# Attention with soft experts on one core: the products p·v done per tile of 128 rows, or once per batch

## The chip, the cores and the metric

The kernel runs on one core of a Trainium2 chip. The metric is the device time of one execution in microseconds, the median of three runs. Everything is in one program: eight batches, one launch.

## The reference, cut to what matters

Two stages follow each other. The first is a retention layer with 8 heads, whose output (576 tokens of 512 values in each of 8 batches) is the input `x` of the second; the second has 4 experts, each an attention head of its own with 64 columns:

```
for e in range(E):                       # E = 4 experts
    q = x @ wq[e]; k = x @ wk[e]; v = x @ wv[e]
    scores = scale * (q @ k.transpose(0, 2, 1))      # causal
    a = exp(scores - max); a /= a.sum(-1) + 1e-09
    ye = a @ v @ wo[e]
    out += (weights of the 2 experts that the gate picks, per token) * ye
```

The change concerns `a @ v`: for each token row the weighted sum of `v` over all tokens up to it, for four experts, in fp32.

## The kernel before, in words

A batch of 576 tokens is cut into five tiles `t` of 128, 128, 128, 128 and 64 rows (`CH`), and for the projections into two ranges `r` (`RNG`): tiles 0 and 1, and tiles 2 to 4. A main loop runs over `n`, one tile of the retention stage in each turn; the tile of the expert stage that a turn works on is `m = n - 6`, so the two stages overlap. In each turn the engines get, in this order:

- the retention products of tile `n` and the end of tile `n - 1` (`qk`, `old`, `own`, `st`: products of 64x64 blocks, four at a time on quarters of the array);
- `scores(m)` (L331, L338): products into PSUM, and `soft`: VectorE subtracts, masks and takes the row maximum (`nm`, L349, L353), ScalarE takes the exponential and its row sum (L357);
- `gates` (L285 to L304), small VectorE instructions once a range, when a range's `vproj` is done;
- `spread(m)`: VectorE and ScalarE scale the rows by sum and gate (L378, L376), and VectorE transposes them in blocks of 32x32 (L382) into `pth`, from where TensorE can stream them;
- `work(n)`: of the table `STEPS` what is due in this turn: the projections `kq0`, `kq1` (`pj`, L230), `v0`, `v1` (`pv`, L255, which also send v through DRAM into the layout `vq`), and the output products `o0`, `o1` (`po`, L430) of the two ranges;
- `values(m - 1)` (L399): for each 32 tokens `j` of the keys, for the two experts `z` in a half and the four 32-row groups `g`, one product with 64 columns of `vq` as the weights and the 32 or 64 columns of one tile of `pth` streamed. Each such product is on the chip two products with their own weight loads, as the others in fp32 are. Eight of them lie on different parts of the array (four row groups, two column halves).

`values` then gathers its four PSUM banks into `y32` (ScalarE L413, VectorE L411), and GpSimd splits that into a rounded part `yh` (L419) and a rest `yl` (L420), which `outproj` reads. For tile `t` there are 32, 64, 96, 128 and 144 products in the program, 464 a batch.

TensorE, VectorE, ScalarE and GpSimd run their instructions in the order in which the program writes them. PSUM is a ring of eight banks taken in that order. Counted by `n`, the five kinds of turn, called steps A to E below, hold:

| step | n | expert tile t | work before | values before |
|---|---|---|---|---|
| A | 5b + 6 | 0 | kq1 of batch b | tile 4 of batch b - 1 |
| B | 5b + 7 | 1 | v1 of b, o1 of b - 1 | tile 0 of b |
| C | 5b + 8 | 2 | kq0 of b + 1 | tile 1 of b |
| D | 5b + 9 | 3 | o0 of b | tile 2 of b |
| E | 5b + 10 | 4 | v0 of b + 1 | tile 3 of b |

After the loop `end` does the last tiles, whose scores, spreads, values and output products follow each other with little else beside them.

Of the kernel before, what the change touches and what calls it, by code (L numbers as in the profile page):

```python
# [8 lines left out]
F32 = mybir.dt.float32  # L9
# [24 lines left out]
def kernel(ctx: ExitStack, tc: tile.TileContext, xf, xt, vkf, vkt,  # L34
# [165 lines left out]
    def fetch(n):  # L200
        o, kc, w = WCUT[n]
        RAW[n] = raw = ld.tile([128, kc, w], F32, name="raw", bufs=3)
        nc.sync.dma_start(raw, wraw[:, o:o + kc * w].rearrange("p (k w) -> p k w", k=kc))
# [105 lines left out]
    SS, PT, YU = {}, {}, {}  # L309
# [52 lines left out]
    def spread(m):  # L362
# [9 lines left out]
        PT[m] = pth = sb.tile([128, ws[-1] // 32, n, 32], F32, name="pth", tag="pth", bufs=2)  # L372
# [12 lines left out]
    def values(m):  # L385
        b, t = divmod(m, 5)
        t0, C = CH[t]
        r = 0 if t < 2 else 1
        r0, n, tiles = RNG[r]
        pth = PT.pop(m)  # L390
        k = C // 64
        nj = (t0 + C) // 32
        py = [bank([128, k, 32], "ys") for g in range(4)]
        for j in range(nj):
            vq, jj = VN[b, 0 if j < 8 else 1][2], j - (0 if j < 8 else 8)
            i0 = 1 if k == 2 and j >= nj - 2 else 0
            for z in range(2):
                for g in range(4):
                    mm(py[g][HALF[z], i0:], vq[QUAD[g], jj, D * z:D * z + D], pth[QUAD[g], j, k * z + i0:k * z + k],  # L399
                       start=(j == 0), stop=(j == nj - 1))  # L400
        if (b, r) not in YU:
            YU[b, r] = (sb.tile([128, 2, n], F32R, name=f"yh{r}", bufs=1),
                        sb.tile([128, 2, n], F32R, name=f"yl{r}", bufs=1))
        yh, yl = YU[b, r]
        l0 = t0 - r0
        hi, lo = yh[:, :, l0:l0 + C], yl[:, :, l0:l0 + C]
        y32 = sb.tile([128, 2, k, 2, 32], F32, name="y32", tag="y32")
        for g in range(4):
            o = y32[:, g // 2, :, g % 2]
            if g % 2:  # L410
                v.tensor_copy(o, py[g])  # L411
            else:
                act(o, py[g], AF.Copy)  # L413
        y32 = y32.rearrange("p a i b c -> p a (i b c)")
        if m == NC - 3:
            act(hi, y32, AF.Copy)
            v.tensor_sub(lo, y32, f(hi))
        else:
            gp.tensor_copy(hi, y32)  # L419
            gp.tensor_sub(lo, y32, f(hi))  # L420

    def outproj(b, r, d):
        r0, n, tiles = RNG[r]
        yh, yl = YU[b, r]
# [15 lines left out]
    for b in range(B):  # L440
        late = b == B - 1

        for n, kind in ((5 * b + 3, "kq0"), (5 * b + 5 - late, "v0"), (5 * b + 6, "kq1"), (5 * b + 7, "v1"),
                        (5 * b + 9 + (b == B - 2), "o0"), (5 * b + 12, "o1")):
            if b or kind[-1] == "1" or kind == "o0":
                STEPS.setdefault(n, []).append((b, kind, None))

# [3 lines left out]
    def work(n):  # L451
        for b, kind, part in STEPS.get(n, []):
            r = int(kind[-1])
# [21 lines left out]
    def end():  # L475
# [4 lines left out]
        values(LAST + 1)  # L480
# [23 lines left out]
    for n in range(NC + 2):  # L504
# [6 lines left out]
        new, old = TILES.get(n, []), TILES.get(n - 1, [])  # L511
# [89 lines left out]
```

## Time and profile before

| | us |
|---|---|
| median of three runs | 598.53 |
| lowest and highest of them | 595.57, 599.73 |
| the profiled execution, its time | 601.69 |
| its span, first to last instruction | 599.8 |
| TensorE products busy in it | 495.3 |
| VectorE busy | 344.3 |
| ScalarE busy | 261.8 |
| GpSimd busy | 213.7 |

The time of an execution is 1.9 us more than the span. Busy time of TensorE is the time in which at least one product is in flight; eight small ones at once count once. The granted clock is the share of its full 2.4 GHz that TensorE gets; it takes two levels, 1.0 and 0.5, and a slice or stretch shows their mean.

### The profile page before, as it was taken

What the parts mean: (1) busy time and instruction counts of PE and PEld (TensorE: products, weight loads), DVE (VectorE), ACT (ScalarE), POOL (GpSimd) and SP (SyncE); (2) the same over time, 40 slices, a digit from 0 to 9 for tenths busy, and PEclk for the clock granted to TensorE, in tenths of its full rate; (3) what the DMA queues carried; (4) which work ended last, traced back from release to release, by engine and by line L of the source; (5) the groups of instructions that cost most, each with busy time, mean ns of one, the idle gap of its engine ahead of it and who ended that gap; (6) DMA issues with size and microseconds to landing.
All of it is one profiled execution on the core that took longest, in us unless ns stands there. A gap on an engine that the chain in (4) does not pass through costs nothing.

```text
span 599.8 us, 31543 instructions
## 1 busy us (share of the span) xinstructions
PE 495.3 (83%) x14060; PEld 438.2 (73%) x14060; DVE 344.3 (57%) x1240; ACT 261.8 (44%) x847; POOL 213.7 (36%) x276
## 2 busy tenths in 40 slices
PE   6789877889878998879878988879878798788855
PEld 3678866887667977769768976779767786676655
DVE  3457875456663587636765578626685268623820
ACT  4265463244532545245633455326542355433421
POOL 3374544133442354425333345424343243101010
PEclk9599998879898898979888799779897799787766
DMA  8674535035340463225342355304532040200411
GB/s 319 232 249 125 149 112 146 17 117 152 111 157 4 141 171 136 91 74 137 141 135 56 107 163 178 91 28 149 166 125 75 4 124 20 74 3 14 113 40 45
DMA packets 49287, 67.38 MB, mean 112 GB/s; under 512 B 4096, under 2 KB 38400, under 8 KB 49152
## 3 DMA queue, kind: packets, MB, share of 16 engines
q1 hardware_dynamic: 49152, 65.38, 34.8%
q8 instruction: 110, 1.80, 1.3%
q14 instruction: 25, 0.20, 0.1%
HBM read 50.68 MB, written 14.68 MB: 109 GB/s over the span
## 4 chain that ended last, share of the span: by engine, by line
PE 62%; DVE 13%; issue 13%; ACT 8%; DMA 2%; POOL 1%; SPq 1%; DVEq 0%; ACTq 0%; POOLq 0%
PE ys L399 13%; PE pj L230 13%; PE pv L255 9%; PE po L430 7%; PE ss L331 6%; ACT p L357 4%; PE own L176 4%; PE qk L135 4%; PE old L163 3%; PE st L115 3%; DVE p L378 2%; DVE pth L382 2%; DMA vk<-vkf 2%; PE ss L338 2%; DVE ex L297 1%
## 5 line engine op out<-in xcount | busy, mean ns | idle before, releaser
L399 PE MATMUL ys<-pth,vq 32*64 32x64 f32 (+1 forms) x7424 | 97.7, 237 | 50.2 <-issue 48.4
L399 PEld LDWEIGHTS ys<-pth,vq 32*64 32x64 f32 x7424 | 89.2, 139 | 59.8 <-issue 55.6
L357 ACT ACTIVATE p<-p,nm 128x64 f32<-128x64 f32 (+6 forms) x144 | 79.5, 553 | 107.8 <-DVE nm L349 80.5
L419 POOL CAST yh<-y 128x256 fp32r<-128x256 f32 (+1 forms) x39 | 14.6, 374 | 222.2 <-DVE y L411 155.1
L382 DVE STREAM_TRANSPOSE pth<-p 128x64 f32<-128x64 f32 (+6 forms) x144 | 61.3, 478 | 13.2 <-PE ys L399 12.9
L376 ACT ACTIVATE p<-p,sm 128x320 f32<-128x320 f32 (+8 forms) x72 | 37.0, 555 | 64.3 <-DVE sm L371 64.3
L181 DVE TENSOR_TENSOR x<-x,own 128x256 f32<-128x256 f32 (+1 forms) x80 | 26.7, 364 | 61.6 <-ACT x L166 27.5
L141 POOL TENSOR_SCALAR_AFFINE_SELECT p<-p 64x512 f32<-64x512 f32 (+1 forms) x80 | 49.8, 622 | 32.5 <-ACT p L138 29.9
L331 PE MATMUL ss<-k,q 64*64 64x448 f32 (+7 forms) x512 | 54.4, 509 | 7.8 <-issue 4.1
L349 DVE CUSTOM_DVE_ANT_0 p<-ss,mask 128x128 f32<-128x128 f32 (+7 forms) x128 | 51.0, 453 | 11.0 <-PE ss L331 10.7
L378 DVE TENSOR_SCALAR p<-p,sm 128x320 f32<-128x320 f32 (+8 forms) x72 | 54.7, 796 | 1.4
L411 DVE COPY y<-ys 128x64 f32<-128x64 f32 (+1 forms) x80 | 13.3, 204 | 69.1 <-PE ys L399 69.0
L186 POOL TENSOR_TENSOR x<-x,gi 128x512 f32<-128x512 f32 (+1 forms) x38 | 44.2, 1162 | 18.7 <-DVE x L181 11.9
L176 PE MATMUL own<-p,vk 64*64 64x64 f32 x1152 | 38.0, 256 | 12.9 <-issue 7.9
L189 POOL TENSOR_TENSOR x1l<-x,x1h 128x512 fp32r<-128x512 f32 (+1 forms) x24 | 26.3, 1097 | 59.0 <-ACT x1h L187 59.0
L413 ACT ACTIVATE y<-ys 128x64 f32<-128x64 f32 (+1 forms) x80 | 13.3, 221 | 77.7 <-PE ys L399 77.6
L135 PE MATMUL qk<-x 64*64 64x64 f32 x1152 | 33.0, 248 | 13.4 <-issue 7.8
L176 PEld LDWEIGHTS own<-p,vk 64*64 64x64 f32 x1152 | 31.8, 165 | 15.4 <-issue 14.6
L135 PEld LDWEIGHTS qk<-x 64*64 64x64 f32 x1152 | 25.8, 153 | 17.7 <-issue 9.3
L138 ACT ACTIVATE p<-qk 128x256 f32<-128x256 f32 (+1 forms) x80 | 24.7, 364 | 31.2 <-PE qk L135 31.1
L331 PEld LDWEIGHTS ss<-k,q 64*64 64x64 f32 x512 | 26.0, 175 | 16.8 <-issue 9.1
L163 PE MATMUL old<-x,s 64*64 64x64 f32 x1024 | 30.1, 248 | 7.1 <-issue 5.8
(107 smaller groups left out, 1070.4 us busy)
## 6 DMA issues: line engine op xcount, KB each, us to landing
x<-xf SPq DMA_DIRECT2D x32, 512.0 KB, 4.1
vk<-vkf SPq DMA_DIRECT2D x32, 512.0 KB, 5.4
vq<-hv SPq DMA_DIRECT2D x32, 192.0 KB, 4.2
out<-ot SPq DMA_DIRECT2D x32, 160.0 KB, 1.9
vq<-hv SPq DMA_DIRECT2D x32, 128.0 KB, 3.1
out<-ot SPq DMA_DIRECT2D x32, 128.0 KB, 2.2
hv<-vn SPq DMA_DIRECT2D x8, 384.0 KB, 3.4
raw<-wraw SPq DMA_DIRECT2D x4, 512.0 KB, 7.7
```

Source lines behind the costliest of these rows:

```text
L135: mm(ps[g][HALF[r], s, u], x[HALF[g], 1, h, i], x[HALF[g], 0, h, i], start=True, stop=True)
L141: gp.affine_select(w, w, pattern=[[0, 4 * k], [1, 64]], base=0, channel_multiplier=-1, compare_op=OP.is_ge, fill=0.0)
L163: mm(old[g][HALF[u], r, i], S_[b, k - 1][HALF[g], r, u], x[HALF[g], 0, 2 * r + u, i], start=True, stop=True)
L176: mm(own[r][HALF[u], g, i], vk[HALF[r], s, 0, 2 * g + u], p[HALF[r], g, s, u], start=True, stop=True)
L230: mm(ps, ww[:, kc, p * 128:(p + 1) * 128], xx[:, kc, :n], start=(i == 0), stop=(i == 11))
L255: mm(ps, xx[:, kc, l0:l0 + 128], ww[:, kc], start=(i == 0), stop=(i == 11))
L331: mm(ps[u][HALF[p]], q[p][HALF[z], l0 + 64 * i:l0 + 64 * i + 64], k[p][HALF[z], :ws[u]], start=True, stop=True)
L349: v.tensor_tensor_reduce(x, ps[u], mask[:, 512 - ws[u]:], -1.0, BIG, OP.add, OP.min, nm[:, u:u + 1])
L357: act(x, x, AF.Exp, bias=bias, scale=-1.0, accum_out=sm[:, 0, u:u + 1])
L378: v.tensor_scalar(x, x, rs[:, u:u + 1], None, op0=OP.mult)
L382: v.transpose(pth[:, :ws[u] // 32, z * (n // 2) + i], p32[:, u, :ws[u]].rearrange("p (j c) -> p j c", c=32))
L399: mm(py[g][HALF[z], i0:], vq[QUAD[g], jj, D * z:D * z + D], pth[QUAD[g], j, k * z + i0:k * z + k], start=(j == 0), stop=(j == nj - 1))
```

## The change

`values` is no longer called per tile. The transposed rows of all five tiles of a batch are kept in two buffers, `TA` (the first 8 blocks of 32 key tokens) and `TB` (the other 10), so a transpose that reaches over block 8 becomes two instructions. There is one buffer of each, and the raw weights are loaded into `TA` before its first use. `values(b, 0, 9)` runs once a batch: for each `j` eight products with the columns of all tiles that see these tokens, 288 at `j = 0`, 32 at `j = 17`, 144 products in all. It stops after `j = 5` and `j = 11`, and `work` puts the three pieces between the four projections of `kq1` of the next batch, in step A. The spread of tile 0 in that step transposes only after them (`hold`). The four banks are evicted by ScalarE straight into `yh` and by VectorE (a subtraction that reads PSUM) into `yl`; `y32` and the two GpSimd instructions are gone. `o0` moves to step B and `o1` to step D. In `end` the last batch is done in two calls, `values(b, 0, 4)` and `values(b, 4, 9)`.

```diff
+    TA = const.tile([128, 8, 2, 9, 32], F32, name="ta")
+    TB = const.tile([128, 10, 2, 5, 32], F32, name="tb")
 ...
         for u in range(n):
-            z, i = u % 2, u // 2
-            v.transpose(pth[:, :ws[u] // 32, z * (n // 2) + i], p32[:, u, :ws[u]].rearrange("p (j c) -> p j c", c=32))
+            z, k, nb = u % 2, 2 * t + u // 2, ws[u] // 32
+            x = p32[:, u, :ws[u]].rearrange("p (j c) -> p j c", c=32)
+            v.transpose(TA[:, :min(nb, 8), z, k], x[:, :min(nb, 8)])
+            if nb > 8:
+                v.transpose(TB[:, :nb - 8, z, k - 4], x[:, 8:])
             yield
 ...
+    def values(b, s0, s1):
+        py = [bank([128, s1 - s0, 32], "ys") for g in range(4)]
+        for j in range(2 * s1):
+            sj = max(s0, j // 2)
+            vq, jj = VN[b, 0 if j < 8 else 1][2], j % 8 if j < 8 else j - 8
             for z in range(2):
+                tt = TA[:, j, z, sj:s1] if j < 8 else TB[:, j - 8, z, sj - 4:s1 - 4]
                 for g in range(4):
+                    mm(py[g][HALF[z], sj - s0:], vq[QUAD[g], jj, D * z:D * z + D], tt[QUAD[g]],
+                       start=(j == 0), stop=(j == 2 * s1 - 1))
+            if j % 6 == 5 and j < 2 * s1 - 1:
+                yield
 ...
         for g in range(4):
+            hi, lo = (y[:, g // 2, s0:s1, g % 2] for y in YU[b])
+            act(hi, py[g], AF.Copy)
+            v.tensor_sub(lo, py[g], f(hi))
+        yield
 ...
-                        (5 * b + 9 + (b == B - 2), "o0"), (5 * b + 12, "o1")):
+                        (5 * b + 11, "y"), (5 * b + 12, "o0"), (5 * b + 14, "o1")):
 ...
                     for w in "kq":
                         yield from proj(b, r, w, p)
+                        for y in vals:
+                            next(y, None)
 ...
+        run(values(b, 0, 4))
         for d in range(4):
             run(outproj(b, 0, d))
-        values(LAST + 3)
         run(spread(LAST + 2))
-        values(LAST + 4)
-        values(LAST + 2)
+        run(values(b, 4, 9))
 ...
+        hold = any(kind == "y" for _, kind, _ in STEPS.get(n, []))
         for _ in work(n):
-            next(spreads, None)
+            if not hold:
+                next(spreads, None)
         run(spreads)
         run(late)
-        for m in old:
-            values(m)
```

TensorE in a step A, from inside its projections on (`pj` the projections, `ys` the products of `values`, a row's x16 is a count of the program, `vq_...` and `x1h`, `whk` are buffers and need not be told apart). Before:

```order
L230 MATMUL pj<-x1h,whk 128x320 x4
L230 MATMUL pj<-x1l,whk 128x320 x4
L230 MATMUL pj<-x1h,wlk 128x320 x4
L230 MATMUL pj<-x1h,whq 128x320 x4
L230 MATMUL pj<-x1l,whq 128x320 x4
L230 MATMUL pj<-x1h,wlq 128x320 x4
L399 MATMUL ys<-pth,vq_6155 64x32 x64
L399 MATMUL ys<-pth,vq_6863 64x32 x80
L135 MATMUL qk<-x 64x64 x16
```

and of the changed kernel, the same place (of another batch):

```order
L233 MATMUL pj<-x1h,whk 128x320 x4
L233 MATMUL pj<-x1l,whk 128x320 x4
L233 MATMUL pj<-x1h,wlk 128x320 x4
L398 MATMUL ys<-ta,vq_5896 64x288 x16
L398 MATMUL ys<-ta,vq_5896 64x256 x16
L398 MATMUL ys<-ta,vq_5896 64x224 x16
L233 MATMUL pj<-x1h,whq 128x320 x4
L233 MATMUL pj<-x1l,whq 128x320 x4
L233 MATMUL pj<-x1h,wlq 128x320 x4
L398 MATMUL ys<-ta,vq_5896 64x192 x16
L398 MATMUL ys<-tb,vq_6424 64x160 x16
L398 MATMUL ys<-tb,vq_6424 64x128 x16
```

Where one block of 144 products with 32 columns stood behind all projections, three blocks of 48 products with 288 down to 32 columns stand between them; the blocks behind the work of steps B to E are gone.

VectorE at the end of a step D and the beginning of step E (the scaling L378 or L380, then the transposes, then the retention stage's additions). Before:

```order
L378 TENSOR_SCALAR p_5870<-p_5870,sm 128x448
L378 TENSOR_SCALAR p_5870<-p_5870,sm 128x512
L382 STREAM_TRANSPOSE pth<-p_5870 128x14x32 x2
L382 STREAM_TRANSPOSE pth<-p_5870 128x16x32 x2
L411 COPY y_6039<-ys 128x2x32 x2
L181 TENSOR_TENSOR x_6075<-x_6075,own 128x2x64 x2
L121 COPY s<-st 128x128 x2
```

and of the changed kernel:

```order
L380 TENSOR_SCALAR p_3540<-p_3540,sm 128x512
L385 STREAM_TRANSPOSE ta<-p_3540 128x8x32
L387 STREAM_TRANSPOSE tb<-p_3540 128x6x32
L385 STREAM_TRANSPOSE ta<-p_3540 128x8x32
L387 STREAM_TRANSPOSE tb<-p_3540 128x6x32
L385 STREAM_TRANSPOSE ta<-p_3540 128x8x32
L387 STREAM_TRANSPOSE tb<-p_3540 128x8x32
L385 STREAM_TRANSPOSE ta<-p_3540 128x8x32
L387 STREAM_TRANSPOSE tb<-p_3540 128x8x32
L183 TENSOR_TENSOR x_3639<-x_3639,own 128x2x64 x2
L123 COPY s<-st 128x128 x2
```

Each of the four transposes is now two, and the two copies out of the four banks of `ys` are gone.

## Rows read from the trace of the kernel before

**Rows 1.** The page of the kernel before: busy us with share of the span and count of instructions of each engine (PE products of TensorE, PEld its weight loads, DVE VectorE, ACT ScalarE, POOL GpSimd), and the granted TensorE clock in 40 slices.

```profile
PE 495.3 (83%) x14060; PEld 438.2 (73%) x14060; DVE 344.3 (57%) x1240; ACT 261.8 (44%) x847; POOL 213.7 (36%) x276
...
PEclk9599998879898898979888799779897799787766
```

**Rows 2.** The groups of instructions by line, whole span: line, engine, operation, what it writes and reads, shapes, count, then busy us and mean ns of one, then the idle time before them and what ended it.

```profile
L399 PE MATMUL ys<-pth,vq 32*64 32x64 f32 (+1 forms) x7424 | 97.7, 237 | 50.2 <-issue 48.4 <-DVE nm L349 1.8
L419 POOL CAST yh<-y 128x256 fp32r<-128x256 f32 (+1 forms) x39 | 14.6, 374 | 222.2 <-DVE y L411 155.1 <-ACT p L138 25.4 <-DVE sm L369 19.5
L420 POOL TENSOR_TENSOR yl<-y,yh 128x256 fp32r<-128x256 f32 (+1 forms) x39 | 26.2, 671 | 3.1
L411 DVE COPY y<-ys 128x64 f32<-128x64 f32 (+1 forms) x80 | 13.3, 204 | 69.1 <-PE ys L399 69.0
```

**Rows 3.** Busy time by stretch, whole span in three pieces (the head up to 52.1 us has no such instruction), of the instructions that write or read the tile `ys` alone. The columns are the stretch in us from the span's start, its length, then for each engine the busy time with the count of instructions, then the granted clock, the DMA share and GB/s.

```profile
52.10:100.30 48.20, 8.36 (x640) 7.64 (x640) 0.96 (x6) 1.03 (x6) 0.96 0.43 131
100.30:498.90 398.60, 64.66 (x5128) 58.98 (x5120) 9.29 (x56) 9.25 (x56) 0.89 0.36 109
498.90:599.80 100.90, 24.71 (x1664) 22.62 (x1664) 3.02 (x18) 3.06 (x18) 0.76 0.15 46
```

**Rows 4.** The timeline of TensorE around the end of a step E (n = 25): start, length from first start to last end, line, operation, shapes and count of products, and in brackets the idle time before.

```profile
305.14 0.91 PE L255 MATMUL pv<-whv,xh 128*128 128x260 f32 x4
305.89 0.64 PE L255 MATMUL pv<-wlv,xh 128*128 128x260 f32 x4
306.37 0.64 PE L255 MATMUL pv<-whv,xl 128*128 128x260 f32 x4
308.37 1.93 PE L399 MATMUL ys<-pth,vq 32*64 32x64 f32 x161
311.94 1.22 PE L399 MATMUL ys<-pth,vq 32*64 32x64 f32 x95 [1.63 <-issue]
```

**Rows 5.** The timeline of TensorE in the last 31 us, same columns.

```profile
569.75 2.60 PE L399 MATMUL ys<-pth,vq 32*64 32x64 f32 x222
574.61 1.87 PE L399 MATMUL ys<-pth,vq 32*64 32x64 f32 x128 [2.26 <-issue]
578.36 2.04 PE L399 MATMUL ys<-pth,vq 32*64 32x32 f32 x128 [1.87 <-issue]
...
590.72 0.87 PE L430 MATMUL po<-yh,who 128*128 128x320 f32 x2 [0.87 <-issue]
```

**Rows 6.** The DMA queue that fetches instructions, from the page: packets, MB, share of 16 engines' span.

```profile
q8 instruction: 110, 1.80, 1.3%
```

**Rows 7.** Busy time of all engines in the six stretches of step A between 100.3 and 471.8 us (two of them and the sum). The columns are the stretch in us from the span's start, its length, then for each engine the busy time with the count of instructions, then the granted clock, the DMA share and GB/s.

```profile
243.30:260.30 17.00, 13.01 (x468) 12.12 (x467) 8.48 (x41) 5.44 (x22) 6.02 (x7) 1.00 0.21 65
...
380.20:400.20 20.00, 15.98 (x472) 14.99 (x464) 8.21 (x41) 5.55 (x22) 5.94 (x7) 0.77 0.19 56
...
sum 113.70, PE 90.66 PEld 85.34 DVE 49.62 ACT 32.96 POOL 35.70; mean PE 15.11 PEld 14.22 DVE 8.27 ACT 5.49 POOL 5.95
```

**Rows 8.** The same for the six stretches of step B (two of them and the sum).

```profile
260.30:276.20 15.90, 14.17 (x272) 13.08 (x268) 7.75 (x28) 7.41 (x24) 5.63 (x7) 0.79 0.34 111
...
471.80:485.80 14.00, 13.69 (x275) 12.96 (x268) 7.76 (x28) 7.40 (x24) 5.64 (x7) 0.84 0.14 49
sum 89.40, PE 84.50 PEld 78.78 DVE 46.63 ACT 44.28 POOL 33.81; mean PE 14.08 PEld 13.13 DVE 7.77 ACT 7.38 POOL 5.64
```

**Rows 9.** The same for steps C, D and E taken together, five times, and for one more step C alone (485.8 to 498.9).

```profile
345.40:380.20 34.80, 28.67 (x1035) 25.16 (x1024) 26.36 (x84) 18.59 (x57) 16.00 (x21) 1.00 0.50 151
...
485.80:498.90 13.10, 11.04 (x329) 9.86 (x321) 9.32 (x37) 5.96 (x20) 5.50 (x7) 1.00 0.36 94
sum 195.50, PE 165.70 PEld 141.70 DVE 141.18 ACT 98.58 POOL 85.37; mean PE 27.62 PEld 23.62 DVE 23.53 ACT 16.43 POOL 14.23
```

**Rows 10.** The chain of work that ended last, step A at 313.1 to 331.2 us, from its projections on: start, us, what.

```profile
318.40 7.60 PE pj L230 x48
326.00 2.46 PE ys L399 x154
328.46 1.79 issue
```

**Rows 11.** Busy time by stretch, the score products of one tile of 64 rows alone (four at a time on quarters of the array, 288 columns each).

```profile
371.29:372.39 1.11, 1.11 (x16) 0.55 (x16) 0.07 (x1) 1.00 0.84 328
```

**Rows 12.** The groups kept apart by shape, columns as in Rows 2: two transposes, an eviction by ScalarE, an addition out of PSUM by VectorE.

```profile
L382 DVE STREAM_TRANSPOSE pth<-p 128x576 f32<-128x576 f32 x16 | 11.6, 760 | 0.3
L382 DVE STREAM_TRANSPOSE pth<-p 128x448 f32<-128x448 f32 x16 | 9.3, 615 | 0.0
L433 ACT ACTIVATE ot<-po 128x320 f32<-128x320 f32 x32 | 11.5, 431 | 4.8 <-PE po L430 4.8
L181 DVE TENSOR_TENSOR x<-x,own 128x256 f32<-128x256 f32 x48 | 18.2, 418 | 51.5 <-PE own L176 26.0 <-ACT x L166 21.8 <-POOL p L141 2.3
```

**Rows 13.** VectorE's waits in steps C to E at 345.4 to 380.2 us: who waited for whom, us in total, times, longest.

```profile
DVE x L181 <- ACT x L166: 2.7, 2, 1.5
DVE sm L369 <- ACT p L357: 2.1, 2, 1.1
DVE x L181 <- PE own L176: 0.9, 2, 0.5
DVE ex L297 <- ACT ex L296: 0.7, 1, 0.7
```

More of the change, by code (lines that the diff above doesn't have):

```diff
@@ L201, in fetch @@
         o, kc, w = WCUT[n]
-        RAW[n] = raw = ld.tile([128, kc, w], F32, name="raw", bufs=3)
+        c = 1024 * "kqvo".index(n)
+        RAW[n] = raw = TA.rearrange("p j z s c -> p (j z s c)")[:, c:c + 1024].rearrange("p (k w) -> p k w", k=kc)
         nc.sync.dma_start(raw, wraw[:, o:o + kc * w].rearrange("p (k w) -> p k w", k=kc))
@@ L305, in gate @@
                              mx[HALF[i], 2].unsqueeze(2).to_broadcast([64, nt, 2]))
-    SS, PT, YU = {}, {}, {}
+    SS, YU = {}, {}
     def scores(m):
@@ L371, in spread @@
         v.tensor_mul(rs, rs, WT[b, r][:, ti].rearrange("p i z -> p (i z)")[:, :n])
-        PT[m] = pth = sb.tile([128, ws[-1] // 32, n, 32], F32, name="pth", tag="pth", bufs=2)
         for u in range(n):
@@ L380, in spread @@
         for u in range(n):
-            z, i = u % 2, u // 2
-            v.transpose(pth[:, :ws[u] // 32, z * (n // 2) + i], p32[:, u, :ws[u]].rearrange("p (j c) -> p j c", c=32))
-            yield
[L385 to L396, printed above, removed]
+            z, k, nb = u % 2, 2 * t + u // 2, ws[u] // 32
@@ L398, in values @@
                 for g in range(4):
[L399 to L406, printed above, removed]
@@ L422, in outproj @@
+            if j % 6 == 5 and j < 2 * s1 - 1:
+                yield
+        if b not in YU:
+            YU[b] = [sb.tile([128, 2, 9, 2, 32], F32R, name=x, bufs=1) for x in ("yh", "yl")]
+        for g in range(4):
+            hi, lo = (y[:, g // 2, s0:s1, g % 2] for y in YU[b])
+            act(hi, py[g], AF.Copy)
+            v.tensor_sub(lo, py[g], f(hi))
+        yield
     def outproj(b, r, d):
         r0, n, tiles = RNG[r]
-        yh, yl = YU[b, r]
+        yh, yl = (y.rearrange("p a s b c -> p a (s b c)")[:, :, r0:r0 + n] for y in YU[b])
@@ L443 @@
         for n, kind in ((5 * b + 3, "kq0"), (5 * b + 5 - late, "v0"), (5 * b + 6, "kq1"), (5 * b + 7, "v1"),
-                        (5 * b + 9 + (b == B - 2), "o0"), (5 * b + 12, "o1")):
-            if b or kind[-1] == "1" or kind == "o0":
+                        (5 * b + 11, "y"), (5 * b + 12, "o0"), (5 * b + 14, "o1")):
+            if b or kind[-1] == "1" or kind in ("o0", "y"):
                 STEPS.setdefault(n, []).append((b, kind, None))
+    for n in STEPS:
+        STEPS[n].sort(key=lambda x: "kvyo".index(x[1][0]))
     for n, kind, part in ((2, "kq0", 0), (3, "kq0", 1), (4, "v0", 0), (5, "v0", 1)):
@@ L451, in work @@
     def work(n):
+        vals = [values(b, 0, 9) for b, kind, part in STEPS.get(n, []) if kind == "y"]
         for b, kind, part in STEPS.get(n, []):
+            if kind == "y":
+                continue
             r = int(kind[-1])
@@ L479, in end @@
             run(vproj(b, 1, t))
-        values(LAST + 1)
+        for d in range(4):
+            run(outproj(b - 1, 0, d))
         gates()
@@ L510 @@
             fetch("v" if n == 1 else "o")
-        new, old = TILES.get(n, []), TILES.get(n - 1, [])
+        new = TILES.get(n, [])
         late = result(n - 1) if 1 <= n <= NC else iter(())
@@ L537 @@
             run(scores(m))
+        new = {NC: new[:1], NC + 1: [LAST] + new}.get(n, new)
         spreads = (None for m in new for _ in spread(m))
         next(spreads, None)
+        hold = any(kind == "y" for _, kind, _ in STEPS.get(n, []))
         for _ in work(n):
-            next(spreads, None)
+            if not hold:
+                next(spreads, None)
         run(spreads)
         run(late)
-        for m in old:
-            values(m)
     end()
```

13 lines of the change are left out of this document (removed).

## The prediction

> **What bounds the kernel now.** I read the page first, then the groups by line, then stretches of busy time by step, then the timeline where TensorE stands still, and VectorE's waits last. The page shows TensorE busy in 83% of the span and VectorE in 57% [rows 1], so TensorE is the first suspect. The costliest group by far is the product of `values`: 97.7 us busy and another 50.2 us idle just before it, of which 48.4 have no releaser but "issue" [rows 2]. Together 148 us for 7,424 products on the chip, 20 ns each.
>
> What that issue time is, the timeline at the end of the kernel shows: blocks of 128 products run in 1.9 to 2.0 us and TensorE stands for 1.9 to 2.3 us between them, with no semaphore involved [rows 5]. 28,120 instructions of TensorE (products and weight loads, [rows 1]) in 110 packets of the instruction queue [rows 6] are 256 a packet, so 128 products with their loads. So TensorE eats one packet of instructions and waits for the next: from start to start 3.75 us for 128, 29 ns a product, whatever its size. Earlier blocks show the same, 1.63 us in a step E [rows 4], 1.79 us in a step A [rows 10]. A kernel with so many tiny products is short of instructions, and the clock suffers for the standstill: the steps A have a clock of 0.77 to 1.00 and last 20.0 us at the one and 17.0 at the other [rows 7].
>
> By steps: A lasts 18.95 us (113.7 / 6) with VectorE busy for 8.3 of it [rows 7], B 14.9 us with VectorE at 7.8 [rows 8]; both hang on TensorE. C, D and E together last 36.5 us ((195.5 - 13.1) / 5), and VectorE is busy for 26.4 [rows 9]. There TensorE's lead is small: in the quietest such triple, 34.8 us at full clock, VectorE was busy for 26.4 and waited for the other 8.4.
>
> **The change part by part.**
>
> *Removed:* 464 products a batch, 928 on the chip. *Added:* 144, so 288 on the chip, and 128 + 288 for the last batch; 7 x 288 + 416 = 2,432 instead of 7,424, and 18,136 instructions of TensorE instead of 28,120, some 71 packets.
>
> *What the new block costs.* Its columns: 288 + 256 + ... + 32 = 1,440, twice, eight products of each, two on the chip for each: 46,080 column passes a batch, exactly as before. Sixteen products of 288 columns, four in flight, took 1.11 us [rows 11], so 0.24 ns a column pass and 0.96 with one in flight. Eight in flight would make 5.5 us a batch, five 8.9, four 11.1. In `values` of before 161 products of 64 columns started and ended within 1.93 us [rows 4], 12 ns each where one alone would take 62: five at once at least, and that block had its packets to wait for. The new ones lie on the same eight parts of the array and their long streams leave the feed time; I take 5.5. The Trainium skill ("TensorE: Matmul & The Clock Gate", Part 1, under "Wait — 56ns, not 53.3ns?") has another price for small products, a floor of about 25 ns from start to start. By it 928 products cost 23.2 us a batch and 288 cost 7.2, a gain of 16 a batch; the 12 ns of the row are under that floor, so the trace does not agree, and I go by the rows.
>
> *Switches.* A projection uses the whole array, and the first group of them behind small products takes longer: 0.75 us from start to start where the next takes 0.48 [rows 4]. Three more such entries a step A make 0.8 us, between 0 and 1.6. The Trainium skill ("TensorEngine Tiling", Key Properties) says that a change of tiling mode drains the engine, which speaks against interleaving; the 0.27 us agree with it.
>
> *Evictions.* ScalarE does four of 288 columns a batch (0.41 us each, under the 431 ns of 320 columns) for ten short ones, VectorE four subtractions (0.45, over the 418 of 256 columns [rows 12]) for ten copies of 0.17 [rows 2]: both even out. They hide behind the last projection of step A, 1.9 us (7.60 / 4, [rows 10]); the next user of the first of these banks is `qk` of step B, and the first pair takes 0.9. Without that cover four pairs would cost up to 3.4 us a batch. GpSimd loses 40.8 us, and I count no gain: it stood idle for 222 us before L419 alone [rows 2]. `o0` and `o1` swap steps and put their output DMAs at the same two places of SP's queue, so I count nothing.
>
> *Transposes.* From 448 to 576 columns a transpose grows by 145 ns [rows 12], 1.13 a column, which leaves 0.11 us fixed. Ten more a batch: 1.1 us on VectorE, all in steps C to E. Those that `hold` puts back are tile 0's four small ones, and nobody wants them before the next batch. The new block's first piece needs tile 4's transposes, the last of step E; TensorE has the retention products, scores and a projection before it, so no wait.
>
> *Step A after.* In the row with the full clock TensorE was busy for 13.0 us [rows 7], some 3.6 of it the values of tile 4 (288 at 64.66 / 5,128 = 12.6 ns, [rows 3]). 13.0 - 3.6 + 5.5 + 0.8 = 15.7 without any wait; 18.95 - 5.8 (288 at 20 ns) + 8.9 + 1.6 = 23.7 with five in flight and the clock as now. I take 16.8, next to the 17.0 of the clean row: -2.15 a step, six steps, -12.9.
>
> *Step B after.* Only 64 products leave it, but the standstill and low clock that it inherits from A's long block go too. Now 14.9 at a clock of 0.79 to 0.84. Its 14.1 busy us times a clock of 0.81 are 11.4 at full clock; less 0.8 for the values 10.6, and some 9.9 if the products that now start late do not. The other end is 14.9 - 0.8 = 14.1. I take 11.2: -3.7, six steps, -22.2.
>
> *Steps C to E after.* VectorE is the bound: 26.4 + 1.1 - 1.0 (six copies) = 26.5 without a wait, 36.5 if it waits as now. Its waits in the quiet triple are 2.7 for ScalarE's copies and 0.9 for products, which come earlier when TensorE has no values before them, and 2.1 and 0.7 for exponentials [rows 13], which stay. I take 31.8, half way: -4.7, five times, and -1.5 for the odd step C, -25.
>
> *Beginning.* 52.1 to 100.3 us is a B, C, D, E with 8.4 us of values [rows 3]: -5.8 by the same shares. The head has none.
>
> *End.* The last block of values is 736 products, 569.75 to 590.72, 21 us [rows 5]; the other 928 of the last 100.9 us [rows 3] at the mean of 20 ns are 18.5, together 39.5. In their place stand 46,080 + 10,240 + 35,840 passes, 11 us, and one for switches. The last tile's scaling and transposes, and a part of the gates, were under the old blocks and lie bare now: 8 us by VectorE's pace there. -19.5; -8 if VectorE's chain is longer, -28 if shorter; I take -19.
>
> Sum: -12.9 - 22.2 - 25 - 5.8 - 19 = -84.9. The profiled execution took 601.7, its span 599.8 plus 1.9, so 516.8 by its measure; it was 3.2 above the median of 598.5, so the median after is 513.6, 514.
>
> **The rivals.**
>
> *VectorE's waits stay.* In C to E the softmax goes VectorE, ScalarE, VectorE, and if the waits hang on that and not on TensorE, the 36.5 us stay. For it speaks that in the quiet triple almost nothing waited for `ys`; against it that its ScalarE waits begin with copies that stand behind the values. Then -12.9 - 22.2 - 0.8 for the beginning, -16 at the end: 598.5 - 52 = 547.
>
> *All waits go.* A 15.7, B 9.9, C to E 26.5, beginning -10, end -28: -19.5 - 30 - 52 - 10 - 28 = -140, 459. Against it: a step's longest engine changes from TensorE to VectorE and back, and eight banks let one run little ahead of the other.
>
> *The clock.* TensorE will stand still in C to E, waiting for VectorE, where it was packed, and come into A and B at the lower level. The triple at 345.4, with TensorE busy in 28.7 of 34.8 us, had a clock of 1.00 [rows 9]; the last 100.9 us, with its standstills, had 0.76 [rows 3]. A at 0.77 took 3 us more than at 1.00 [rows 7], B at its present clock is 2 above my 11.2: 5 us a batch, six batches, 598.5 - 85 + 30 = 544. The Trainium skill ("TensorE: Matmul & The Clock Gate", Why this matters for your kernels) warns of just that, idle gaps between bursts that return the engine to half rate; the row of step A agrees, and the change opens such gaps.
>
> *Slower: long streams do not share the array.* One column pass with one in flight is 0.96 ns, so 46,080 are 44 us a batch; the old blocks took 18.5 (148 / 8). Below 2.4 products in flight the new block costs more than all the old ones; with one, 26 us a batch more, 8 x 26 = 205 slower, some 800. Four in flight were seen [rows 11] and five deduced, so this is unlikely, but eight streams of 288 columns at once no row shows.
>
> **How the numbers follow.** Forecast 0.54 (its own range 495 to 532), waits stay 0.16, clock 0.16, all waits go 0.10, slower 0.04. From 486 (between forecast and all waits gone) to 547 (the two dearer cases, to their middle) some 0.8. A measurement of this kernel can tell 1% from no change. Faster by over 1%: 0.95; within 1%: 0.01; slower: 0.04.
>
> **What would show it right or wrong.** After: some 71 instruction packets; no issue stall in B to E; `ys` at 2,432 products and some 45 to 55 us busy; B at 11 us and a clock near 1; VectorE over 65% busy; its waits for `own` and ScalarE's copies halved. Wrong: steps C to E still at 36 us; a mean clock under 0.87; the new block over 9 us a batch; `qk` of step B waiting for the evictions.

## The result, and the profile after

The changed kernel takes 507.09 us (median of four runs, 504.59 to 509.4), the kernel before 598.53 beside it (median of three, 595.57 to 599.73): ratio 0.848, 95% interval 0.8416 to 0.8543. A fourth execution of the kernel before, 665.81 us, fell in a slower state of the chip and is left out. The forecast was 514 us, with 486 to 547 as its range. The profiled execution took 509.4 us with a span of 507.7, against 599.8 before.

The page after, the same lines as [rows 1, 6]:

```profile
PE 434.3 (86%) x9068; PEld 375.5 (74%) x9068; DVE 343.8 (68%) x1275; ACT 258.7 (51%) x802; POOL 174.8 (34%) x198
...
PEclk9579997799998999989988999989988998979879
...
q8 instruction: 71, 1.16, 1.0%
```

VectorE is busy for as long as before; TensorE for 61.0 us less (495.3 to 434.3), at a mean clock of 0.92 where it was 0.87. The packets of instructions are the 71 that were counted out. The groups that answer to [rows 2]:

```profile
L398 PE MATMUL ys<-ta,vq 32*64 32x256 f32 (+8 forms) x1152 | 34.7, 369 | 3.8 <-DVE ta L385 2.0 <-issue 1.8
L398 PE MATMUL ys<-tb,vq 32*64 32x128 f32 (+4 forms) x1280 | 20.8, 258 | 0.9 <-issue 0.9
```

55.5 us busy and 4.7 idle before them stand where 97.7 and 50.2 stood. The other 18.8 us of busy time went from lines whose products did not change, while the mean clock rose. The rest of the difference is in TensorE's waits. Who TensorE waited for, us in total, times, longest, in the kernel before:

```profile
PE ys L399 <- issue: 48.4, 31, 2.5
PE own L176 <- issue: 7.9, 6, 2.8
PE qk L135 <- issue: 7.8, 5, 2.0
```

and after:

```profile
PE st L117 <- POOL vk L104: 14.7, 6, 4.8
PE own L178 <- ACT k L238: 14.0, 8, 1.9
PE st L117 <- POOL p L143: 7.0, 2, 3.6
...
PE own L178 <- issue: 3.2, 2, 3.0
PE ys L398 <- issue: 2.7, 2, 1.8
```

Added up over the whole of this view, TensorE's waits fell from 100.9 to 70.0 us: those for "issue" from 76.9 to 5.9, while the others, for VectorE, ScalarE and GpSimd, rose from 24.0 to 64.1. So the 92.1 us of span are, to 0.2, 61.0 of busy time (42.2 of them at `ys`) and 71.0 of waits for instructions, less 40.1 that came back as other waits.

That "issue" means the feed of instructions in the kernel before can be counted. In its trace 44 such waits are longer than 0.7 us, 73.3 us of the 76.9. From one of them to the next TensorE runs 126, 253, 127, 377, 253, 256 ... products: 39 of the 43 distances are within 8 of a multiple of 128, half a packet of 256 instructions.

By steps, the answers to [rows 7, 8, 9]: one step A and the sum of six, one step B and the sum of six, one C to E, the odd C and the sum of five with the odd C, then the end and the beginning. Columns are the stretch, its length, then TensorE's products, its loads, VectorE, ScalarE and GpSimd, each busy us with count, then clock, DMA share, GB/s.

```profile
326.40:346.60 20.20, 17.83 (x469) 15.40 (x468) 12.52 (x50) 8.54 (x29) 6.58 (x7) 0.92 0.27 76
...
sum 124.40, PE 107.96 PEld 94.16 DVE 75.26 ACT 51.40 POOL 39.50; mean PE 17.99 PEld 15.69 DVE 12.54 ACT 8.57 POOL 6.58
...
346.60:356.80 10.20, 10.20 (x205) 9.68 (x204) 7.75 (x31) 6.92 (x22) 4.90 (x5) 1.00 0.41 140
...
sum 61.70, PE 61.70 PEld 58.42 DVE 46.74 ACT 41.58 POOL 29.44; mean PE 10.28 PEld 9.74 DVE 7.79 ACT 6.93 POOL 4.91
...
299.40:326.40 27.00, 22.99 (x453) 19.63 (x452) 21.77 (x78) 15.37 (x47) 11.04 (x13) 1.00 0.63 185
...
414.90:424.00 9.10, 9.10 (x193) 8.23 (x192) 6.25 (x25) 4.62 (x15) 4.44 (x5) 1.00 0.65 152
sum 145.80, PE 128.90 PEld 108.89 DVE 115.83 ACT 81.58 POOL 59.61; mean PE 21.48 PEld 18.15 DVE 19.31 ACT 13.60 POOL 9.93
...
424.00:507.70 83.70, 66.89 (x1157) 55.21 (x1156) 47.37 (x195) 39.41 (x117) 4.84 (x6) 0.88 0.21 61
54.10:92.10 38.00, 28.68 (x605) 24.34 (x604) 31.22 (x114) 20.92 (x66) 16.04 (x18) 0.91 0.49 144
```

| piece | before | after | difference | forecast |
|---|---|---|---|---|
| head | 52.1 | 54.1 | +2.0 | 0 |
| beginning | 48.2 | 38.0 | -10.2 | -5.8 |
| six steps A | 113.7 | 124.4 | +10.7 | -12.9 |
| six steps B | 89.4 | 61.7 | -27.7 | -22.2 |
| C to E, five, and one C | 195.5 | 145.8 | -49.7 | -25 |
| end | 100.9 | 83.7 | -17.2 | -19 |
| span | 599.8 | 507.7 | -92.1 | -84.9 |

The sum is right, two of its terms are not: A got longer, and C to E gave twice what was expected.

### The profile page after: what moved, and what is told of

Read it like the earlier page. It is cut to its first block, busy times and chain, and to the rows that moved or that the text cites. A ratio compares the mean times of both kernels' runs of the same rounds, so it can differ in the third digit from the quotient of the medians.

```text
span 507.7 us, 21336 instructions
## 1 busy us (share of the span) xinstructions
PE 434.3 (86%) x9068; PEld 375.5 (74%) x9068; DVE 343.8 (68%) x1275; ACT 258.7 (51%) x802; POOL 174.8 (34%) x198
## 5 line engine op out<-in xcount | busy, mean ns | idle before, releaser
L143 POOL TENSOR_SCALAR_AFFINE_SELECT p<-p 64x512 f32<-64x512 f32 (+1 forms) x80 | 50.1, 626 | 152.2 <-ACT p L140 149.5
L378 ACT ACTIVATE p<-p,sm 128x320 f32<-128x320 f32 (+8 forms) x72 | 36.9, 555 | 62.7 <-DVE sm L374 62.7
L380 DVE TENSOR_SCALAR p<-p,sm 128x320 f32<-128x320 f32 (+8 forms) x72 | 54.2, 789 | 1.4
L385 DVE STREAM_TRANSPOSE ta<-p 128x256 f32<-128x256 f32 (+2 forms) x144 | 49.8, 368 | 4.4 <-ACT p L378 4.1
L188 POOL TENSOR_TENSOR x<-x,gi 128x512 f32<-128x512 f32 (+1 forms) x38 | 44.3, 1166 | 22.4 <-DVE x L183 17.6
L183 DVE TENSOR_TENSOR x<-x,own 128x256 f32<-128x256 f32 (+1 forms) x80 | 26.1, 358 | 38.1 <-ACT x L168 37.9
L334 PE MATMUL ss<-k,q 64*64 64x512 f32 (+7 forms) x512 | 48.2, 470 | 2.3 <-DVE nm L356 1.6
L191 POOL TENSOR_TENSOR x1l<-x,x1h 128x512 fp32r<-128x512 f32 (+1 forms) x24 | 26.4, 1099 | 65.6 <-ACT x1h L189 65.6
L407 DVE TENSOR_TENSOR yl<-ys,yh 128x288 fp32r<-128x288 f32 (+2 forms) x36 | 12.8, 416 | 52.1 <-ACT yh L406 52.1
L117 PE MATMUL st<-vk 64*64 64x64 f32 x1024 | 26.1, 232 | 24.4 <-POOL vk L104 14.7
L117 PEld LDWEIGHTS st<-vk 64*64 64x64 f32 x1024 | 22.1, 143 | 26.3 <-POOL vk L104 15.4
L398 PE MATMUL ys<-ta,vq 32*64 32x256 f32 (+8 forms) x1152 | 34.7, 369 | 3.8 <-DVE ta L385 2.0
L398 PEld LDWEIGHTS ys<-ta,vq 32*64 32x64 f32 x1152 | 25.6, 141 | 12.2 <-issue 6.9
L104 POOL TENSOR_TENSOR vk<-vk,con 128x512 f32<-128x512 f32 (+1 forms) x34 | 33.4, 984 | 0.1
L418 PE MATMUL po<-yh,who 128*128 128x320 f32 (+1 forms) x128 | 29.6, 312 | 3.3 <-ACT yh L406 3.3
L421 ACT ACTIVATE ot<-po 128x256 f32<-128x256 f32 (+1 forms) x64 | 24.0, 407 | 15.4 <-PE po L418 12.3
```

Source lines behind the costliest of these rows:

```text
L117: mm(ps[r][HALF[g], s, u], vk[HALF[r], s, 1, h], vk[HALF[r], s, 0, h], start=True, stop=True)
L143: gp.affine_select(w, w, pattern=[[0, 4 * k], [1, 64]], base=0, channel_multiplier=-1, compare_op=OP.is_ge, fill=0.0)
L188: e.tensor_mul(x32, x32, gi[:, :, t0:t0 + C])
L334: mm(ps[u][HALF[p]], q[p][HALF[z], l0 + 64 * i:l0 + 64 * i + 64], k[p][HALF[z], :ws[u]], start=True, stop=True)
L378: act(x, x, AF.Copy, scale=rs[:, u:u + 1])
L380: v.tensor_scalar(x, x, rs[:, u:u + 1], None, op0=OP.mult)
```

## The experiments

Each was timed in turns with the kernel before on the same chip; the ratio is to that kernel.

**The number of products, with columns and place held.**

```diff
-                for g in range(4):
-                    mm(py[g][HALF[z], sj - s0:], vq[...], tt[QUAD[g]],
 ...
+                for a in range(0, s1 - sj, 2):        # at most 64 columns
+                    e = min(a + 2, s1 - sj)
+                    for g in range(4):
+                        mm(py[g][HALF[z], sj - s0 + a:sj - s0 + e], vq[...], tt[QUAD[g], a:e],
 ...
```

> The changed kernel, with each product of the new block cut into pieces of at most 64 columns: 400 program products a batch instead of 144, the same columns, places on the array, weights and order of the pieces. Theory 'number': what the change saved is the number of instructions, since TensorE gets 256 of them and then waits for the next packet (29 ns a product with its load in the kernel before). Then 256 more program products, 512 on the chip, a batch cost up to 14.8 us if all were exposed, and about half of it since the block stands among long projections: 40 to 100 us slower than the changed kernel, 550 to 605 us, with issue idle before ys of 20 us or more. Theory 'place' (the gain is from doing the values once a batch, away from the steps where VectorE bounds): the columns and the place are the same, so the time stays within 10 us of 507, whatever the number.

602.85 us, 1.012 (1.0054 to 1.0185): all of the gain is gone, and a little more. C to E last 26.9 us as in the changed kernel; the loss stands where `ys` stands, in A (20.7 to 33.5 us) and the end. TensorE in a step A, start, length, products and the idle time before:

```profile
390.00 1.76 PE L400 MATMUL ys<-ta,vq 32*64 32x64 f32 x128 [1.59 <-issue]
393.47 1.30 PE L400 MATMUL ys<-ta,vq 32*64 32x64 f32 x87 [1.71 <-issue]
```

The picture of [rows 5] is back: 128 products in 1.76 us, 14 ns each, then a standstill for the next 256 instructions. The span is 96.2 us longer for 4,032 more products on the chip, 23.9 ns each. About half of that is time in which TensorE is busy (434.3 to 482.9 us), the other half waits (70.0 to 117.3 us in all, those for issue 5.9 to 47.8). The number is the price, not the place and not the columns.

**The same small products, handed out among long ones**, in the kernel before:

```diff
+            if j and j % cut == 0:
+                yield
 ...
         for _ in work(n):
             next(spreads, None)
+            next(vals, None)
```

> The kernel before, with its values still per tile and of 32 or 64 columns, 464 products a batch, but handed out in pieces between the projections and output products of the same step instead of behind them. Theory 'rate': the 48 us of issue idle before ys come only because small products stand in a row; among long products the packets come in time, and so most of the 48 us go: 550 to 570 us. Theory 'number': the same instructions and packets are needed, so what is saved at one place is paid at another: 585 to 600. A part of the gain may be eaten by entries to projections, 0.3 us each, some 20 more a batch, 40 us: then 590 to 610.

567.04 us, 0.9488 (0.94 to 0.9576), as the theory of the rate has it. The group of `ys`:

```profile
L402 PE MATMUL ys<-pth,vq 32*64 32x64 f32 (+1 forms) x7424 | 131.5, 238 | 18.2 <-issue 17.6
```

As many products as before, but 17.6 us of issue idle instead of 48.4. Not all of that is saved: over the whole kernel the waits for issue fell by 52 us (76.9 to 24.9), and TensorE's busy time rose by 21 (495.3 to 516.3), with `ys` in flight for 131.5 us instead of 97.7. Still, a third of the change's gain could be had without saving one product.

**The block in one stretch.**

```diff
-                        for y in vals:
-                            next(y, None)
 ...
+                for y in vals:
+                    yield from y
```

> The changed kernel, with the three pieces of the new block not among the projections but in one stretch behind them. Theory 'switches': three fewer entries from small products to projections a batch, 0.8 us each batch less, 6 us faster at most, 500 to 507. Theory 'cover': 288 chip products with loads need 576 instructions, more than two packets, and the four pairs of evictions then stand bare in front of the next retention products, about 2 to 3.5 us a batch: 15 to 28 us slower, 522 to 535, with a wait of qk's products for the eviction at the start of step B.

516.1 us, 0.866 (0.861 to 0.871), 9 us more than in three pieces; "cover" has the sign, at less than it asked, and of its two reasons only the first. TensorE behind a step A's projections:

```profile
349.08 3.50 PE L398 MATMUL ys<-ta,vq 32*64 32x288 f32 x128
352.38 2.30 PE L398 MATMUL ys<-tb,vq 32*64 32x160 f32 x160
354.61 0.32 PE L137 MATMUL qk<-x 64*64 64x64 f32 x3
356.11 0.63 PE L137 MATMUL qk<-x 64*64 64x64 f32 x27 [1.18 <-issue]
```

From 349.08 to 354.61 are 5.53 us for the whole block: the 5.5 estimated, all eight parts at work. It is the quickest of six; the others take 5.68 to 6.82. What follows isn't a wait for the evictions, as I had expected, but for instructions: it falls behind the third product of `qk`, and in the trace the next one waits for no semaphore. All waits for issue are 15.2 us here, 5.9 with three pieces.

**The evictions alone**, straight from PSUM, in the kernel before:

```diff
-            o = y32[:, g // 2, :, g % 2]
 ...
-            gp.tensor_copy(hi, y32)
-            gp.tensor_sub(lo, y32, f(hi))
+            act(hi[:, g // 2, :, g % 2], py[g], AF.Copy)
+            v.tensor_sub(lo[:, g // 2, :, g % 2], py[g], f(hi[:, g // 2, :, g % 2]))
```

> The kernel before, with one part of the change alone: ScalarE evicts the banks of values straight into the rounded part yh and VectorE subtracts from PSUM into yl; y32 and GpSimd's two instructions are gone, values stay per tile. Theory 'free' (the forecast's): GpSimd's 40.8 us were hidden, so the time stays within 6 us of 598. Rival 'latency': the path from the last product to the output products gets shorter by GpSimd's two instructions and the end gains, 5 to 15 us faster; or VectorE, the bound of C to E, gets longer instructions and 5 to 15 us are lost.

594.69 us, 0.9949 (0.9897 to 1.0002): GpSimd's 40 us less and VectorE's longer instructions (351.9 us busy for 344.3) are together worth nothing that can be told from zero.

**What values cost before and after.** In each only the first and the last `j` are left.

```diff
-        for j in range(nj):          # kernel before
+        for j in (0, nj - 1):
-        for j in range(2 * s1):      # changed kernel
+        for j in (0, 2 * s1 - 1):
```

> The kernel before, with only the first and the last 32 keys of each tile's values: 80 program products a batch instead of 464, the others left out, all else as it was. It shows what the products of values cost before, all waits included. By the rows 148 us stand at ys, 0.83 of them go: 123 us, to 475, if nothing takes their place. If VectorE's chain bounds C to E at nearly what they took, only A, B and the end gain: 530 to 545. I expect 490.

> The changed kernel, with only the first and the last j of the block: 16 program products a batch instead of 144, the others left out. It shows what the block still costs. By the columns it takes 5.5 us a batch and its 0.89 of that go, 35 to 40 us with the end: 468 to 475, if TensorE alone sets the length of step A. If step A is held up by what VectorE and ScalarE bring over from C to E, the block stands in time that is lost anyway: 490 to 507.

490.04 us (0.8221, 0.816 to 0.8282) and 469.6 (0.7865, 0.7801 to 0.7929). So 384 of the 464 products a batch cost 107 us before, and 128 of the 144 cost 37.5 now: 70 of the change's 91 us are in the products left out here. The 20 us between these two kernels have another cause, the next question. C to E still last 32.4 us in the first of them.

**Banks or copies**, in the kernel before with few products:

```diff
-        py = [bank([128, k, 32], "ys") for g in range(4)]
+        py = [bank([128, k, 32], "ys")] * 4
 ...
-                for g in range(4):
+                for g in range(1):
```

> The kernel before with hardly any products of values, as in e5_before_few, and only one PSUM bank taken for a tile's values instead of four (only the products of the first row group are left, 20 a batch; the same four evictions all read that one bank). e5_before_few still needed 32 us for C to E where the changed kernel needs 27. Theory 'banks': per-tile values take four of the ring's eight banks in every step, and so the next step's qk, old and own wait for older evictions (qk for ScalarE's copies of k 17 us, old for VectorE's lg 11 us in e5_before_few); with one bank C to E fall to 27 or 28 and the time to 465 to 475. Rival 'evictions': the copies themselves and their place in ScalarE's and VectorE's queues hold things up; then the time stays within 6 us of 490.

488.64 us, 0.8206 (0.8129 to 0.8283): one bank for four gains nothing. That does not clear the banks, because the edit brought in something else. With one bank the four copies of a tile wait for each other, ScalarE's for VectorE's and the other way round (us in total, times, longest):

```profile
ACT y L413 <- DVE y L411: 39.1, 40, 2.5
DVE y L411 <- ACT y L413: 21.4, 50, 2.3
```

The kernel with four banks has neither wait, so what the free banks gave may have gone there. Then with copies for two tiles of five:

```diff
+        if t not in (1, 3):
+            return
```

> The kernel of e10_one_bank, with the banks of values copied out only for tiles 1 and 3 of a batch instead of all five (8 copies a batch instead of 20, and no products for the other three tiles; GpSimd still splits for all five). Theory 'copies in the queue': each turn's copies stand on ScalarE and VectorE behind the transposes of their own turn and ahead of the next turn's v, k and x, and that, not the products, is what a per-tile values costs beyond them; then the wait 'own for lg' and 'st for p' go and the time falls from 489 to 468 to 478, near the 470 of the changed kernel with few products. Rival 'another edit' (the places of o0 and o1, the transposes held back, or the two transpose buffers make the 19 us): it stays at 483 to 490.

474.73 us, 0.7969 (0.7905 to 0.8034), 13.9 less. The few products of the three other tiles went too, 0.35 us a tile or 8.4 us over eight batches if all stood on the path, so three tiles' copies, together with their banks and with their waits for each other, are worth 5.5 to 13.9 of the 20. The sums of the six steps A and of C to E, one bank:

```profile
sum 76.40, PE 65.53 PEld 61.64 DVE 66.87 ACT 32.65 POOL 41.06; mean PE 10.92 PEld 10.27 DVE 11.15 ACT 5.44 POOL 6.84
...
sum 168.40, PE 140.54 PEld 117.31 DVE 126.93 ACT 90.94 POOL 80.95; mean PE 23.42 PEld 19.55 DVE 21.15 ACT 15.16 POOL 13.49
```

and few copies:

```profile
sum 92.00, PE 70.47 PEld 66.63 DVE 68.47 ACT 34.27 POOL 56.68; mean PE 11.74 PEld 11.10 DVE 11.41 ACT 5.71 POOL 9.45
...
sum 149.30, PE 129.57 PEld 107.89 DVE 116.04 ACT 83.77 POOL 70.33; mean PE 21.59 PEld 17.98 DVE 19.34 ACT 13.96 POOL 11.72
```

C to E lose 19.1 us and A gains 15.6 (the beginning is another 5.4 shorter), with a wait of 3.6 us in each step A (`own`, put down to `lg`). This is the pattern of the change itself: where TensorE is freed in C to E, it runs on until the start of A and stands there.

**What it stands for in A.** The decay written earlier, so that it isn't behind GpSimd's other work:

```diff
+        if n > 5:
+            decay(n + 1)
         for m in new[:1]:
             run(scores(m))
```

> The changed kernel, with GpSimd's decay products of the next tile written ahead of the scores and the end of the turn, so that they no longer stand behind GpSimd work that waits for VectorE. Theory 'backlog' (TensorE stands at the start of step A for what VectorE and GpSimd have not done in C to E, seen as st's wait of 2.4 us for the decay): that wait goes, 14.7 us over six steps, and its low clock behind it, 10 to 25 us faster, 482 to 497. Theory 'VectorE bounds': the wait for the decay goes but TensorE then waits for the next thing that VectorE does late, within 5 us of 507.

491.92 us, 0.8252 (0.8198 to 0.8305), 15 us better, but not by its theory: the standstill at `st` stayed and only lost its name.

```profile
316.65 0.70 PE L117 MATMUL st<-vk 64*64 64x64 f32 x32 [2.88 <-issue]
```

VectorE there, the end of tile 4's transposes and what follows:

```profile
316.04 0.47 DVE L387 STREAM_TRANSPOSE tb<-p 128x320 f32<-128x320 f32 x1
316.43 0.19 DVE L263 COPY lg<-pv 128x4 f32<-128x4 f32 x2
```

The 14.7 us of the expectation were also not six steps A, but four of them at 2.3 to 2.4 us, one wait of 4.8 in the beginning and one of 0.4 ahead of it; the other two steps A, 3.4 and 3.6 us, stand in the view as waits for `p` L143.

The same place in the changed kernel, TensorE, ScalarE and GpSimd in one stretch of the timeline each:

```profile
327.11 0.66 PE L178 MATMUL own<-p,vk 64*64 64x64 f32 x32
330.14 0.85 PE L117 MATMUL st<-vk 64*64 64x64 f32 x30 [2.37 <-POOL vk L104]
```

```profile
328.45 0.77 ACT L378 ACTIVATE p<-p,sm 128x576 f32<-128x576 f32 x1 [0.91 <-DVE sm L374]
329.13 0.64 ACT L262 ACTIVATE vn<-pv 128x256 f32<-128x256 f32 x2
329.66 0.66 ACT L140 ACTIVATE p<-qk 128x256 f32<-128x256 f32 x2
```

```profile
328.30 1.04 POOL L104 TENSOR_TENSOR vk<-vk,con 128x512 f32<-128x512 f32 x1
```

GpSimd, named as the releaser, was done at 329.34, 0.80 us before `st` began. ScalarE was copying `qk` out of PSUM just then, and those copies stand in its queue behind the scaling of tile 4 (L378), which waited for VectorE. The semaphores that `st` waits for, by their times in the trace, say the same: the last to come is ScalarE's, at 330.05, with the end of the first of the two copies. In two of the six steps A, and at the row of the early decay above (316.56), it is VectorE's, with the copy `lg` (L263) out of `pv`, which stands behind tile 4's transposes. Either way a copy out of PSUM stands behind tile 4's spread. So the next kernel puts tile 4's spread behind the `qk` of step A, with the decay still early:

```diff
             if n < NC:
                 qk(n)
+            run(held)               # the spread of tile 4
             next(late, None)
```

> The changed kernel with the decay written earlier (as in e7_decay), and the spread of tile 4 put off from the end of step E to behind the products qk of step A. Theory 'bank': st of step A stands 2.4 to 2.9 us because the PSUM bank that it gets is still to be evicted (v by ScalarE and VectorE's L263, or qk by ScalarE), and these stand in their engines' queues behind the scaling and transposes of tile 4. With these behind the evictions the wait at st goes in all six steps A, the clock stays at 1.00 there, and A falls from 19.3 to 16.5 or 17: 12 to 18 us faster than e7_decay, 474 to 480. Rival 'feed': that wait, always about 2.4 us, is one for instructions; it stays and the time is that of e7_decay, 487 to 497. Rival 'transposes': the wait goes at st and comes back at the first product of the new block, which wants tile 4's transposes: 485 to 492.

481.59 us, 0.807 (0.8016 to 0.8124). The wait at `st` is down to 0.32, and the clock is 1.00 in all six steps A:

```profile
362.06 0.85 PE L117 MATMUL st<-vk 64*64 64x64 f32 x30 [0.32 <-issue]
```

```profile
360.30:378.40 18.10, 17.27 (x465) 14.89 (x464) 11.05 (x49) 8.57 (x29) 5.74 (x6) 1.00 0.30 86
sum 107.00, PE 102.89 PEld 88.92 DVE 65.91 ACT 50.00 POOL 33.66; mean PE 17.15 PEld 14.82 DVE 10.98 ACT 8.33 POOL 5.61
```

A is 17.8 us, between "bank" (16.5 to 17) and what it was; the gain over the decay alone, 10.3 us, is a little under the 12 asked. Some 0.9 us of the wait came back at the block, as the rival "transposes" had it in place though not in cause: its first piece takes 3.67 us to the next projection here, 2.78 in the changed kernel's steps at full clock. Its products wait for VectorE's additions out of PSUM (L183, L125), which now stand behind tile 4's transposes.

> The kernel of e9_late_spread, with the spreads of tiles 2 and 3 put behind the next step's qk as well, as that of tile 4. Theory 'ScalarE's queue': own of step D waits 1.8 us for ScalarE's copy of k, which stands behind the scaling of tile 2; that goes, some 12 us, and E's wait for GpSimd's x1l (1.06 us, behind ScalarE's x1h) may stay: 466 to 474. Rival 'VectorE bounds': VectorE's chain of C to E is as long as before and only begins later, the time goes to E or A: 478 to 487.

Here only the condition changes, from `n > 5 and n % 5 == 0` to `n > 7 and n % 5 in (0, 3, 4)`. 479.5 us, 0.8048 (0.7973 to 0.8123), not to be told from the kernel above; D falls (8.8 to 6.7 us) and E rises (7.9 to 9.75): VectorE's chain.

**The same two edits on the kernel before:**

> The kernel before, values per tile, with the two edits of e7_decay and e9_late_spread: decay written earlier, the spread of tile 4 behind the qk of step A. Theory 'made by the change' (the changed kernel's wait in step A arises because TensorE now runs ahead in C to E; before it was late itself and found VectorE's work done): 0 to 8 us faster than before, 590 to 599. Rival 'was there before': it gains what it gains in the changed kernel, 20 us or more: 570 to 580.

592.86 us, 0.9957 (0.9916 to 0.9998). What is worth 25 us after the change was worth about 3 before it: the change made what these edits remove. Not all of that need be the standstill, since they also shorten VectorE's busy time, by 20.9 us in the changed kernel (343.8 to 322.9) and by 19.0 in the one before (344.3 to 325.3), where it hardly counted.

## Why the prediction was right, and where its steps were not

*Instructions bound the small products: right, and larger than counted.* The forecast saw 48.4 us of issue at `ys`. There were 76.9 of it in all, since the standstill also fell on the `own`, `qk` and `old` that come next, and 5.9 are left. Narrow products bring 47.8 back, and the time with them.

*The block, 5.5 us: right.* 5.53 in the quickest single stretch, 5.9 to 6.3 in three pieces. The rival of streams that do not share the array is out.

*The rule of the Trainium skill on small products: nearer than I said.* ("TensorE: Matmul & The Clock Gate", Part 1, "Wait — 56ns, not 53.3ns?": no less than some 25 ns from start to start.) The rows of inside a packet still disagree, 128 products in 1.76 us; the price over a whole kernel, 23.9 ns a product, is close to it, but half of that price is the standstill between packets.

*Switches, 0.27 us each: too dear, by a misread row.* In the part of [rows 4] that gave 0.75 and 0.48 us the clock rose: it was 0.50 from 303.0 to 305.1 us and 1.00 from 305.9. At full clock the changed kernel shows 0.70 and then 0.58, 0.12 an entry and some 0.4 a step A instead of 0.8:

```profile
341.42 0.86 PE L233 MATMUL pj<-x1h,whk 128*128 128x320 f32 x4
342.12 0.75 PE L233 MATMUL pj<-x1l,whk 128*128 128x320 f32 x4
342.70 0.74 PE L233 MATMUL pj<-x1h,wlk 128*128 128x320 f32 x4
```

*B, 11.2 us: 10.3,* with TensorE busy throughout and a clock of 1.00, 0.79 and 0.84 in the steps of [rows 8]; "the products that now start late do not" was its other end, 9.9.

*C to E and A: the sum right, both terms wrong.* Forecast 31.8 + 16.8 = 48.6 us a batch; measured 27.3 + 20.7 = 48.0. The failing step is the 26.5 us of VectorE's work that C to E were given as their bound, beside an A "without any wait" at a clean clock. Only 21.9 us of that work stand in C to E now ((115.83 - 6.25) / 5), 26.4 before. That VectorE's idle time there would halve was right: 10.1 us before, 5.4 after, 5.3 forecast. But 4.3 us of VectorE's work are now done when TensorE is already in A, 12.5 us there for 8.3: 1.1 of them are the block's evictions, the rest mostly tile 4's scaling and transposes. Behind those TensorE stands at the start of A. The standstill costs twice, 2.3 to 3.6 us and the half clock that the rows of A show after it (0.92 instead of 1.00; at 327 to 335 us, 2.4 us of standstill and then a clock of 0.50 from 331.7 to 335.1). With the spread moved, A is 17.8 at 1.00, 1.0 over the 16.8. I had asked whether the new block would wait for tile 4's transposes and found that it would not; it didn't, but the copies out of PSUM behind tile 4's scaling and transposes, ScalarE's and VectorE's, were queues that I hadn't followed.

*The evictions "both even out": right for their busy time* (450 ns for VectorE's of 288 columns, 417 for ScalarE's) *and for GpSimd; their number I had not priced.* Twelve fewer copies a batch stand in the queues of C to E, with their banks. With few products twelve fewer were worth 5.5 to 13.9 us; I had counted 1 us a batch of VectorE's busy time.

*The end, -17.2 for -19, right; the beginning, -10.2 for -5.8,* undercounted like C to E, of which it has one.

*The rivals.* "VectorE's waits stay" fell: C to E are 27.3, not 36.5. "All waits go" has its number in C to E, 26.5, but not its reason: 5.4 us of VectorE's idle time stay there. "The clock" came true in A alone, at 0.92 where it had 0.77; B, two of its five us a batch, ran at 1.00.

*The signs.* Packets (71), busy time of `ys` (55.5), B, VectorE's share (68%) and the mean clock came as forecast, and VectorE's waits for `own` all but went (44.4 to 0.8 us). Its waits for ScalarE's copies of `old` did not halve: 27.5 us before, 37.9 after.

*Open:* of the 20 us between the two kernels with few products, three tiles' copies and banks, not told apart, are 5.5 to 13.9; the rest, the places of `o0` and `o1` or the transposes held back, was not tried by itself. Nor is it settled how the early decay alone gained 15 us; in that profile E fell from 8.15 to 7.3 us and A from 20.7 to 19.3. In E VectorE's busy time fell by as much as the step, from 7.8 to 6.9 us, so there its shorter instructions can be the whole of it.

## What to carry to other kernels

Count TensorE's instructions, not only its columns: where small products stand in a row, add up every wait for issue, also on the lines behind them, and either widen the products or put long ones between. When the bound of a stretch goes, sum the stretch with its neighbours: the engine that was late runs on to the next thing that the other engines owe, and there the order in their queues (a copy out of PSUM behind a long scaling) is worth more than their busy time. A releaser that was done long before the waiting engine moved isn't the cause; look at what ended just then, and move that.

## What was not expected of the hardware

The same instruction of VectorE takes very different times. Tile 4's scaling (L380, 576 columns) took 1.26 us in the changed kernel, where GpSimd's L104 ran beside it, and 0.52 with the decay moved away, GpSimd idle. It is 1.26 in all six turns of the loop and 0.52 in the two that fall in the end, where GpSimd is idle too:

```profile
328.39 1.26 DVE L380 TENSOR_SCALAR p<-p,sm 128x576 f32<-128x576 f32 x1
```

```profile
314.40 0.52 DVE L380 TENSOR_SCALAR p<-p,sm 128x576 f32<-128x576 f32 x1
```

VectorE's busy time over the kernel fell from 343.8 to 328.5 us with the decay early, and to 322.9 with the spread late, for the same 1,275 instructions. That GpSimd's work beside it makes VectorE's instruction longer is what these rows suggest; it was not measured apart.
